# Attention with a relative bias, then a two-layer network: a change to the planner that writes out the order of the work

## The chip, the cores and the metric

The kernel runs on one core of a Trainium2 chip. The metric is device time in microseconds (us); lower is better. The engines are TensorE (PE in the profile, its weight loads PEld), VectorE (DVE), ScalarE (ACT), GpSimd (POOL) and SyncE (SP), which issues DMA transfers and computes nothing. Each has its own queue and works it off in order; semaphores tie them together.

## The reference, cut to what matters

```python
scores = scale * np.matmul(q, k.transpose(0, 1, 3, 2))     # q, k, v: 8 x 8 x 576 x 64
scores = scores + bias.transpose(2, 0, 1)[None, :, :, :]   # from a table of 32 buckets, by |i - j|
scores = scores - np.max(scores, axis=-1, keepdims=True)
attn = np.exp(scores)
attn = attn / (np.sum(attn, axis=-1, keepdims=True) + 1e-09)
out = np.matmul(attn, v)
x = np.ascontiguousarray(out.transpose(0, 2, 1, 3)).reshape(B * S, H * D)   # 4608 x 512
h = x @ w_in                                               # 512 x 2048
g = np.maximum(0.01 * h, h)
return (g @ w_out).astype(np.float32)                      # 2048 x 512
```

## The kernel before, in words

**Pairs.** Two heads of one batch are a pair; 8 batches make 32 pairs, numbered n = 0 to 31. For each pair, q and k (96 x 768 each, loaded by POOL's queue as bf16) must stand with the head's 64 numbers along the partitions, so they are turned. There are three ways. Pair 0 and pairs 5 to 7: `rows` (L362) copies the rows of both heads side by side into a tile `pr` (four buffers), six PE transposes for q and six for k turn it (`turn_by_pe`, L376), and `take_turned` (L393) copies the result from PSUM to `qt` and `kt`. Pairs 1 to 4: PE turns straight from the loaded rows (L381). From pair 8 on, `by_dma(n)` is true: `turn_by_dma` (L367) lets SP issue one DMA transpose from `pr` to `tu` for q and k together, and `take_turned` copies from `tu`, on DVE.

**Attention of a pair.** `score` (L418 to L426) makes six units of scores in PSUM, in two buffers `ps_s`; `expo` on ACT takes exp (L432, L434, L439); `band` on DVE multiplies the five blocks by the exp of the bias (L451); `av` (L471, L486, L489) multiplies by v with a column of ones; `norm` on DVE (L498, L499) divides into `opair`. The result is turned into `xT`, by PE (`x_pe`, L513, and a DVE copy `x_copy`, L517) for pairs 0 to 5 and two others, and by DMA (`x_dma`, L505, on SP) for the rest.

**The network.** Tokens go in nine blocks of 512. `ffn_in` (L529) makes 16 units of hidden values in PSUM tiles `pm`, ACT applies the leaky ReLU (L533), `ffn_out` (L557) multiplies by w_out, DVE copies (L562) and SP stores (L567). The PSUM pool M has three banks, and `pm`, one output of `av` (`ps_om`), and PE's transposes share it. The network's work is spread between the attention's, so that PE has something to do while ACT and DVE work on a pair.

**Who sets the order.** All engines run in an order written out when the program is built, by class `Plan`. Each piece of work is a task with an engine, a reckoned cost, a list of tasks that it comes after, a rank, and the PSUM slots that it takes and gives. `Plan.order` walks through a reckoned time: for each engine it finds the tasks that could start, takes the earliest (PE, before 34 us, may take a better rank that starts 0.3 us later), and notes start and end. A DMA transpose was reckoned to end 6 us after its issue (`tail=6.0`), whatever else the DMA rings carry; POOL's loads are reckoned to land one behind the other (`ring`). `Plan.run` then emits the tasks in that order, and, where PE is reckoned to be idle in the first 26 us, puts multiplications of a zero tile between (`spin`, L781), four of them ahead of all. The reckoned times go nowhere else: on the chip, only the order and the true data dependencies hold.

**Loads.** POOL issues the loads. Batches share two buffers, so the load of q and k of batch b comes after the rows of batch b - 2 were read, and in POOL's queue the order is: q and k of batch 2, v of batch 2, q and k of batch 3, v of batch 3, and so on; v of batch b comes after the last `av` of batch b - 2.

Of the kernel before, what the change touches and what calls it, by code (L numbers as in the profile page):

```python
# [36 lines left out]
class Plan:  # L37


    LAG, WARM, EARLY, PATIENCE = 0.25, 26.0, 34.0, 0.3  # L40

    def __init__(self, slots):
        self.tasks = []
# [3 lines left out]
    def add(self, engine, cost, after, go, rank, take=(), give=(), tail=0.0, at=None):  # L47
        t = {"engine": engine, "cost": cost, "after": list(after), "go": go, "rank": rank, "n": len(self.tasks),
             "take": list(take), "give": list(give), "tail": tail, "end": at, "start": at}
        if at is None:  # L50
            self.tasks.append(t)
        return t
# [8 lines left out]
    def order(self):  # L61

        free, done, waiting, ring = {}, [], {}, 0.0
        for t in self.tasks:
            waiting.setdefault(t["engine"], []).append(t)
        while any(waiting.values()):
            best = None
            for e, ts in waiting.items():
                now = free.get(e, 0.0)
                ready = []  # L70
                for t in ts:
                    if any(d["end"] is None for d in t["after"] + t["behind"]):
                        continue
                    r = now
                    for d in t["after"]:
                        r = max(r, d["end"] + (self.LAG if d["engine"] != e else 0.0))
                    for k in set(t["take"]):
                        s, m = sorted(self.slots[k]), t["take"].count(k)
                        r = max(r, s[m - 1]) if len(s) >= m else None
                        if r is None:  # L80
                            break
                    if r is None:
                        continue
                    ready.append((r, t["rank"], t["n"], t))
                if ready:
                    r = min(ready)[0]
                    slack = self.PATIENCE if e == "PE" and r < self.EARLY else 0.0
                    pick = min((rank, n, s, t) for s, rank, n, t in ready if s <= r + slack) if slack else None
                    pick = (pick[2], pick[0], pick[1], pick[3]) if pick else min(ready)
                    if best is None or pick[:3] < best[:3]:  # L90
                        best = pick
            assert best is not None, [(e, len(w)) for e, w in waiting.items()]
            r, t = best[0], best[3]
            e = t["engine"]
            waiting[e].remove(t)
            t["start"], t["end"] = r, r + t["cost"] + t["tail"]
            if "moves" in t:
                t["end"] = ring = max(ring, r + t["cost"] + 2.0) + t["moves"]
            t["idle"] = r - free.get(e, 0.0)
            free[e] = r + t["cost"]  # L100
            for k in t["take"]:
                self.slots[k].remove(min(self.slots[k]))
            for k in t["give"]:
                self.slots[k].append(t["end"] + self.LAG)
            done.append(t)
        return done

    def run(self, fill):

        for t in self.order():  # L110
            if t["engine"] == "PE" and 3.6 < t["start"] < self.WARM:
                k = int((t["idle"] - 0.3) / (0.45 if t["start"] < 8.0 else 0.25))
                if k > 0:
                    fill(k)
            t["go"]()
# [3 lines left out]
def kernel(  # L119
# [18 lines left out]
    n_pairs = H // 2  # L138
# [117 lines left out]
    spare = extra[:, 0 : ATW + SL], extra[:, ATW + SL : ATW + SL + S + SL]  # L256
# [86 lines left out]
    qts, kts, opairs, prs, turned, scores, outs = {}, {}, {}, {}, {}, {}, {}  # L343

    def by_dma(n):
        return n >= 2 * n_pairs

    def rows_by_pool(n):
        return False
# [4 lines left out]
    def rows(n, j):  # L354

        b, p = items[n]
        if j == 0:
            prs[n] = pr_pool.tile([RQ, 2, NC, 2 * D], BF16, name="pr")
        src = raw[:, j, :, :].rearrange("r e (c d) -> r e c d", d=D) if n == 0 else \
            (qn, kn)[j][b % NBUF][0:RQ, 2 * p : 2 * p + 2, :, :]  # L360
        copy = nc.scalar.copy if n + j == j == 1 else (nc.gpsimd if rows_by_pool(n) else nc.vector).tensor_copy
        copy(out=prs[n][:, j, :, :].rearrange("r c (e d) -> r c e d", e=2),  # L362
                        in_=src.rearrange("r e c d -> r c e d"))

    def turn_by_dma(n):
        t = turned[n] = tu_pool.tile([P, 2 * NC, RQ], BF16, name="tu")
        nc.sync.dma_start_transpose(out=t, in_=prs.pop(n).rearrange("r j c d -> r (j c d)"))  # L367
# [142 lines left out]
    def x_pe(n):  # L510
        ps = outs[n, "x"] = ps_m_pool.tile([P, 8 * P], BF16, name="ps_tx", tag="m")
        for ic in range(NJ + 1):
            nc.tensor.transpose(ps[:, ic * P : (ic + 1) * P], in_=opairs[n][:, ic, :], identity=ident)  # L513

    def x_copy(n):
        b, p = items[n]
        nc.vector.tensor_copy(out=xT[p][:, b * S : (b + 1) * S], in_=outs.pop((n, "x"))[:, 0:S])  # L517
# [52 lines left out]
    add = plan.add  # L570
    L = {}
    rowt, cut, sct, ext, avt, nrt, nmt, xt, vt = {}, {}, {}, {}, {}, {}, {}, {}, {}
# [52 lines left out]
    def plan_rows(n):  # L625
        b, p = items[n]
        rank = 10 * n
        feed = rank - (25 if n < n_pairs else 0)
        ld = None if n == 0 else (L["qk", 0, p - 1] if b == 0 else L["qk", b, p // 2])
        old = [t for t in rowt.get(n - 4, [])[2:]] + (nrt[n_pairs - 1] if n == n_pairs + 1 else [])  # L630
        on, cost = ("POOL", 0.9) if rows_by_pool(n) else ("DVE", 0.35)
        if n == 0:
            r0 = add("DVE", 0.6, [L["raw", 0]], lambda: rows(0, 0), feed)
            r1 = add("ACT", 0.75, [L["raw", 1]], lambda: rows(0, 1), feed)
        elif by_heads(n):
            r0 = r1 = ld
        else:
            r0 = add(on, cost, [ld] + old, lambda: rows(n, 0), feed)
            r1 = add(on, cost, [ld, r0], lambda: rows(n, 1), feed)
        wait = [("in", 0, 1)] if n == n_pairs + 1 else (sct[n - 2][-1:] if n > n_pairs + 1 else [])  # L640
        if by_dma(n):
            d = add("SP", 0.1, [r0, r1] + cut.get(n - 4, [])[:2], lambda: turn_by_dma(n), rank, tail=6.0)
            rowt[n] = [r0, r1, d]
            src, give = [d, d], []
        else:
            g = [add("PE", 0.4 if by_heads(n) else 0.28, [(r0, r1)[j]] + sct.get(n - NQT, []) + wait, lambda j=j: turn_by_pe(n, j), feed, take=["M"])
                 for j in range(2)]
            rowt[n] = g if by_heads(n) else [r0, r1] + g
            src, give = g, ["M"]
        behind = ext[n - 1] if n == n_pairs else []  # L650
        on_act = n < n_pairs - 1 or n_pairs <= n < 2 * n_pairs
        cq = add("ACT" if on_act else "DVE", 0.6 if on_act else 0.75, [src[0]] + behind + sct.get(n - NQT, []),
                 lambda c=nc.scalar.copy if on_act else nc.vector.tensor_copy: take_turned(n, 0, c), feed, give=give)
        on_act = n == n_pairs
        ck = add("ACT" if on_act else "DVE", 0.6 if on_act else 0.75, [src[1]] + behind + sct.get(n - NQT, []),
                 lambda: take_turned(n, 1, nc.scalar.copy if n == n_pairs else nc.vector.tensor_copy), feed, give=give)
        on, cost = ("POOL", 0.5) if 0 < n < n_pairs else ("DVE", 0.2)
        ak = add(on, cost, [ck], lambda: apart(n, kts[n]), feed + 1 if n != 1 else -7)
        aq = add(on, cost, [cq], lambda: apart(n, qts[n]), feed + 1 if n != 1 else -7)
        cut[n] = [cq, ck, aq, ak]  # L660
# [6 lines left out]
    def plan_pair(n):  # L667
        b, p = items[n]
        rank = 10 * n
# [41 lines left out]
        if x_by_dma(n):  # L711
            xt[n] = [add("SP", 0.1, nms, lambda: x_dma(n), soon + 4, tail=6.0)]
            nmt[n] = xt[n]
        else:
            xt[n] = [add("PE", 0.3, nms, lambda: x_pe(n), soon + 4, take=["M"])]
            nmt[n] = [add("DVE", 0.45, xt[n], lambda: x_copy(n), soon + 3, give=["M"])]

    def plan_loads(b):
# [59 lines left out]
    def spin(k):  # L778
        pw = ps_w_pool[0]
        for _ in range(k):  # L780
            nc.tensor.matmul(pw, lhsT=junk[:, 0:P], rhs=junk, start=True, stop=True)  # L781

    ps_w_pool = [ps_m_pool.tile([P, 512], FP32, name="ps_w", tag="m")]
    spin(4)
    plan.run(spin)


# [28 lines left out]
```

## Time and profile before

| What | Value |
|---|---|
| median of three runs | 382.77 us (382.54, 382.77, 387.25) |
| the profiled execution | 388.05 us |
| its span, first to last instruction | 386.1 us |
| PE busy | 370.4 us, 96% |
| ACT busy | 244.7 us, 63% |
| DVE busy | 205.6 us, 53% |
| mean granted TensorE clock | 0.991 |

The profiled execution is longer than its span by 1.95 us, and longer than the median by 5.28 us. In the views below, "timeline" rows give start and duration in us, engine, line, operation, output<-inputs, shapes, count, and in brackets the engine's idle time before and what ended it. A q behind an engine's name marks its queue's issue of a DMA.

### The profile page before, as it was taken

The page shows a single profiled execution, that of the slowest core. Times are in us where ns is not written, and L with a number is a line of the kernel's source. Part 1 is how long each engine was busy: PE and PEld are TensorE (multiplying, and loading weights), DVE is VectorE, ACT ScalarE, POOL GpSimd, SP SyncE. Part 2 cuts the span into 40 slices and gives each one's busy share as a digit, 9 for nine tenths or more (in the row PEclk, how much of TensorE's full clock was granted, in tenths as well). Part 3 has the DMA queues.
Part 4 walks back from the last instruction along what each step waited for, and adds up shares of the span by engine and source line. Part 5 has one row for each costly group of instructions (what it writes and reads, how often), then busy time and mean ns, then how long its engine had stood idle before and what let it go on. Part 6 is the DMA issues. An engine that isn't in the chain of part 4 may idle for free.

```text
span 386.1 us, 8513 instructions
## 1 busy us (share of the span) xinstructions
PE 370.4 (96%) x3469; PEld 191.2 (50%) x3509; DVE 205.6 (53%) x538; ACT 244.7 (63%) x352; POOL 80.2 (21%) x125
## 2 busy tenths in 40 slices
PE   8979999799799999999999999999999999999996
PEld 4547455454344455555555454555454644444444
DVE  7788566685666765757565656555534411001011
ACT  5877996459565798579758775877687533333300
POOL 8994732061003400510060004000000000000000
PEclk9989999999999999999999999999999999999999
DMA  8699999999936993997499839411111100101112
GB/s 153 134 201 220 206 195 143 184 117 159 167 64 114 151 176 58 106 200 122 55 117 152 140 80 107 76 46 44 47 46 44 47 29 27 56 27 42 41 54 82
DMA packets 95046, 40.82 MB, mean 106 GB/s; under 512 B 74304, under 2 KB 88928, under 8 KB 95008
## 3 DMA queue, kind: packets, MB, share of 16 engines
q0 software_dynamic: 44672, 19.24, 43.6%
q1 hardware_dynamic: 50128, 20.75, 27.4%
q8 instruction: 27, 0.44, 0.5%
q10 hardware_dynamic: 208, 0.29, 0.3%
q14 instruction: 11, 0.09, 0.1%
HBM read 36.70 MB, written 9.44 MB: 120 GB/s over the span
## 4 chain that ended last, share of the span: by engine, by line
PE 89%; DVE 6%; DMA 3%; issue 1%; ACT 0%; POOL 0%; POOLq 0%
PE pm L529 33%; PE pm L557 29%; PE ps_s L418 9%; PE ps_om L486 5%; PE ps_o L486 5%; DMA tu<-pr 3%; PE ps_s L422 2%; PE ps_s L425 2%; DVE at L451 1%; PE pm L541 1%; DVE kt L393 1%; PE ps_o L471 1%; PE ps_t L381 1%; PE ps_tx L513 1%; DVE opair L499 1%
## 5 line engine op out<-in xcount | busy, mean ns | idle before, releaser
L432 ACT ACTIVATE at<-ps_s 128x1024 bf16<-128x1024 f32 x124 | 121.0, 1033 | 36.8 <-PE ps_s L418 35.9
L529 PE MATMUL pm<-xT,w_in_sb 128*128 128x512 bf16 x550 | 140.2, 382 | 4.2 <-DVE opair L499 2.8
L557 PE MATMUL pm<-w_out_sb,gt 128*128 128x512 bf16 x549 | 133.6, 379 | 0.6
L533 ACT ACTIVATE gt<-pm 128x512 bf16<-128x512 f32 x144 | 84.3, 610 | 64.9 <-PE pm L529 62.0
L451 DVE TENSOR_TENSOR at<-at,hk 128x768 bf16<-128x768 bf16 (+3 forms) x155 | 70.0, 465 | 33.8 <-ACT at L432 27.0
L529 PEld LDWEIGHTS <-w_in_sb 128*128 128x128 bf16 x576 | 52.7, 98 | 68.3 <-issue 9.1
L557 PEld LDWEIGHTS <-gt 128*128 128x128 bf16 x560 | 52.4, 98 | 64.4 <-issue 4.7
L562 DVE COPY y<-pm 128x512 f32<-128x512 f32 x35 | 24.1, 689 | 70.0 <-PE pm L557 70.0
L199 POOL DMA_DIRECT2D vn<-in_v_dram x24 | 21.9, 940 | 145.5 <-PE ps_o L486 140.4
L418 PE MATMUL ps_s<-qt,kt 64*128 64x512 bf16 x256 | 42.1, 397 | 3.3 <-DVE kt L393 2.6
L486 PEld LDWEIGHTS <-at 128*128 128x128 bf16 x1240 | 41.6, 98 | 3.4 <-issue 1.5
L434 ACT ACTIVATE at<-ps_s 128x512 bf16<-128x512 f32 x31 | 18.6, 599 | 16.4 <-PE ps_s L422 11.5
L393 DVE COPY qt<-tu 128x576 bf16<-128x576 bf16 x24 | 16.9, 704 | 20.4 <-PE ps_s L426 11.0
L486 PE MATMUL ps_o<-vn,at 128*128 128x65 bf16 x640 | 25.8, 195 | 0.0
L486 PE MATMUL ps_om<-vn,at 128*128 128x65 bf16 x600 | 24.4, 195 | 0.3 <-issue 0.3
L498 DVE RECIPROCAL rcp<-ps_om 128x5 f32<-128x5 f32 x31 | 6.0, 195 | 33.0 <-PE ps_om L486 31.8
L418 PEld LDWEIGHTS <-kt 64*128 64x128 bf16 x256 | 8.3, 94 | 29.0 <-issue 24.9
L439 ACT ACTIVATE at<-ps_s 128x576 bf16<-128x576 f32 x31 | 20.3, 656 | 1.2 <-PE ps_s L426 1.0
L393 DVE COPY kt<-tu 128x576 bf16<-128x576 bf16 x24 | 17.0, 707 | 0.0
L499 DVE TENSOR_TENSOR opair<-ps_o,rcp 128x320 bf16<-128x320 f32 x33 | 16.2, 492 | 1.1
L499 DVE TENSOR_TENSOR opair<-ps_om,rcp 128x320 bf16<-128x320 f32 x31 | 15.2, 491 | 1.1
L191 POOL DMA_DIRECT2D kn<-in_k_dram x17 | 12.7, 747 | 5.3 <-DMA w_in_sb<-in_moe_w_in_dram 3.0
(98 smaller groups left out, 254.4 us busy)
## 6 DMA issues: line engine op xcount, KB each, us to landing
out_dram<-y SPq DMA_DIRECT2D x35, 256.0 KB, 2.0
qn<-in_q_dram POOLq DMA_DIRECT2D x14, 288.0 KB, 9.8
kn<-in_k_dram POOLq DMA_DIRECT2D x14, 288.0 KB, 11.5
vn<-in_v_dram POOLq DMA_DIRECT2D x24, 128.0 KB, 5.2
w_in_sb<-in_moe_w_in_dram POOLq DMA_DIRECT2D x2, 1024.0 KB, 11.9
w_out_sb<-in_moe_w_out_dram POOLq DMA_DIRECT2D x2, 1024.0 KB, 14.2
staged<-in_v_dram POOLq DMA_DIRECT2D x4, 256.0 KB, 12.1
first<-in_v_dram POOLq DMA_DIRECT2D x4, 192.0 KB, 4.6
```

The source lines that it names most:

```text
L199: nc.gpsimd.dma_start(out=vn[i][:, c, :, 0:D], in_=v[b, :, c * P : (c + 1) * P, :].rearrange("h s d -> s h d"),)
L393: copy(out=t[:, 0:S].rearrange("p (r c) -> p r c", c=NC), in_=src)
L418: nc.tensor.matmul(ps[:, e, :], lhsT=kt[r, u * P : (u + 1) * P], rhs=qt[r, 0:512], start=True, stop=True)
L432: nc.scalar.activation(at[:, :, u, 0:512], ps, AF.Exp, scale=scale)
L439: nc.scalar.activation(at4[:, 0:S], ps.rearrange("p e i -> p (e i)")[:, 0:S], AF.Exp, scale=scale)
L451: nc.vector.tensor_tensor(out=o, in0=o, in1=m, op=ALU.mult)
L486: nc.tensor.matmul(ps[:, ic, :], lhsT=at[:, o : o + P], rhs=vn[i][:, c, 2 * p + e, :], start=whole and c == 0, stop=not whole and ic == NJ ...
L499: nc.vector.tensor_tensor(out=opairs[n][:, :, e * D : (e + 1) * D], in0=ps[:, :, 0:D], in1=rcp.to_broadcast([P, NJ + 1, D]), op=ALU.mult)
L529: nc.tensor.matmul(pms[T, f], lhsT=w_in_sb[:, c, f * P : (f + 1) * P], rhs=xT[c][:, t0 : t0 + w], start=(c == 0), stop=(c == n_cc - 1))
L533: nc.scalar.activation(gts[T][:, f, :], pms.pop((T, f)), AF.Prelu, bias=0.0, scale=1.0, alpha=0.01)
L557: nc.tensor.matmul(ys[T, ts], lhsT=gts[T][:, f, ts * P : (ts + 1) * P], rhs=w_out_sb[:, f, :], start=(f == 0), stop=(f == n_fc - 1))
L562: nc.vector.tensor_copy(out=y, in_=ys[T, ts])
```

## The change

Six edits, all in the planner and in the tasks given to it. No arithmetic is changed.

1. Pair 8 is no longer turned by DMA: `by_dma` starts at pair 9, so pair 8 takes twelve PE transposes and two copies from PSUM.
2. A DMA transpose is marked `turns`. Its reckoned end is no longer issue + 6.1 us but the loads' reckoned last landing + 2 us, held between 4.5 and 11 us after the issue. The copies of a turned pair also come after a unit of the scores two pairs earlier (`behind`).
3. For pairs turned by DMA, the `rows` copies get a rank 40 lower (`early`), so they are put further ahead.
4. PE's transposes of the outputs of pairs 0 to 2 (`x_pe`) are reckoned ready 1.2 us later (`spare`).
5. PE's tasks that start before 7 us are reckoned at 1.8 times their cost (`COLD`).
6. The filling: five multiplications of the zero tile ahead of all instead of four, and another formula for their number before 8.5 us.

```diff
-    LAG, WARM, EARLY, PATIENCE = 0.25, 26.0, 34.0, 0.3
+    LAG, COLD, WARM, EARLY, PATIENCE = 0.25, 7.0, 26.0, 34.0, 0.3
...
-                        r = max(r, d["end"] + (self.LAG if d["engine"] != e else 0.0))
+                        r = max(r, d["end"] + (self.LAG + t.get("spare", 0.0) if d["engine"] != e else 0.0))
...
-            t["start"], t["end"] = r, r + t["cost"] + t["tail"]
+            cost = t["cost"] * (1.8 if e == "PE" and r < self.COLD else 1.0)
+            t["start"], t["end"] = r, r + cost + t["tail"]
+            if "turns" in t:
+                t["end"] = max(r + 4.5, min(ring + 2.0, r + 11.0))
...
-            if t["engine"] == "PE" and 3.6 < t["start"] < self.WARM:
-                k = int((t["idle"] - 0.3) / (0.45 if t["start"] < 8.0 else 0.25))
+            if t["engine"] == "PE" and 3.9 < t["start"] < self.WARM:
+                k = round(t["idle"] / 0.45) if t["start"] < 8.5 else int((t["idle"] - 0.3) / 0.25)
...
     def by_dma(n):
-        return n >= 2 * n_pairs
+        return n >= 2 * n_pairs + 1
...
+        early = rank - 40 if by_dma(n) else feed
...
-            r0 = add(on, cost, [ld] + old, lambda: rows(n, 0), feed)
-            r1 = add(on, cost, [ld, r0], lambda: rows(n, 1), feed)
+            r0 = add(on, cost, [ld] + old, lambda: rows(n, 0), early)
+            r1 = add(on, cost, [ld, r0], lambda: rows(n, 1), early)
...
             d = add("SP", 0.1, [r0, r1] + cut.get(n - 4, [])[:2], lambda: turn_by_dma(n), rank, tail=6.0)
+            d["turns"] = True
...
-        behind = ext[n - 1] if n == n_pairs else []
+        behind = ext[n - 1] if n == n_pairs else (sct[n - 1][:1] if n == 2 * n_pairs + 1 else sct[n - 2][1:2] if by_dma(n) else [])
...
             xt[n] = [add("PE", 0.3, nms, lambda: x_pe(n), soon + 4, take=["M"])]
+            if n < n_pairs - 1:
+                xt[n][0]["spare"] = 1.2
...
-    spin(4)
+    spin(5)
```

What this makes of the queues, in the program as built:

- **PE, start.** Five zero multiplications instead of four ahead of the bias table's first matmul (L295), three instead of two behind it; then 16 matmuls of the bias table (L311), pair 0's twelve transposes, and 32 more matmuls of the table, where 32 stood ahead of the transposes and 16 behind. Pair 2's k is turned ahead of the fourth score unit of pair 0, not behind its fifth.
- **PE, outputs of pairs 0 to 2.** `x_pe` of pair 0 stood ahead of score units 3 and 4 of pair 2, and now stands behind them; those of pairs 1 and 2 also come later.
- **PE, pair 8.** Its transposes stand behind the first two score units of pair 7.
- **DVE.** The rows of pair 9 stand ahead of those of pair 8. `take_turned` of pair 8 moves ahead of `band` 0 of pair 7. `take_turned` of pair 9 stands behind the last `band` of pair 7. The rows of pairs 12 to 15 move from the time of `band` 0 to 4 of pair 9 to that of pair 8 and the beginning of pair 9. `take_turned` of pair 12 stands behind `band` 1 of pair 10, where it stood ahead of `band` 0 of pair 10; for the later pairs q's copy stands ahead of, and k's behind, `norm` and `band` 2 of a pair.
- **SP.** One DMA transpose fewer; those of pairs 12 to 15 stand earlier among the stores.
- **POOL.** The memsets for batch 1's v stand ahead of its load instead of behind.

More of the change, by code (lines that the diff above doesn't have):

```diff
@@ L99, in order @@
             t["idle"] = r - free.get(e, 0.0)
-            free[e] = r + t["cost"]
+            free[e] = r + cost
             for k in t["take"]:
```

## The prediction

> **What bounds the kernel now.** I read the page's busy times and its chain that ended last, then PE's waits, then the timeline around each long wait, then windows around the dips of the clock.
>
> ```profile
> PE 370.4 (96%) x3469; PEld 191.2 (50%) x3509; DVE 205.6 (53%) x538; ACT 244.7 (63%) x352; POOL 80.2 (21%) x125
> PE 89%; DVE 6%; DMA 3%; issue 1%; ACT 0%; POOL 0%; POOLq 0%
> ```
>
> PE is busy 96% of the span and makes 89% of the chain: a microsecond counts only if PE loses it. What PE waits for is in its waits (total, times, longest):
>
> ```profile
> PE pm L529 <- DVE opair L499: 2.8, 1, 2.8
> PE ps_s L418 <- DVE kt L393: 2.6, 2, 2.1
> PE ps_tx L513 <- DVE opair L499: 2.1, 1, 2.1
> ```
>
> Three waits of over 2 us, each happening once. The clock adds to two of them (stretch, length, then PE, PEld, DVE, ACT, POOL busy, PEclk, DMA share and rate):
>
> ```profile
> 22.69:26.10 3.41, 1.58 (x13) 0.91 (x15) 3.38 (x11) 2.04 (x3) 3.33 (x6) 1.00 1.12 206
> 26.10:29.51 3.41, 3.39 (x42) 2.26 (x41) 2.14 (x7) 2.34 (x4) 3.31 (x7) 0.50 1.12 211
> 70.47:73.88 3.41, 2.24 (x15) 0.91 (x12) 0.87 (x2) 1.14 (x2) 0.00 (x0) 1.00 1.31 167
> 101.20:104.61 3.41, 0.84 (x4) 0.41 (x5) 3.34 (x13) 0.99 (x2) 0.00 (x0) 1.00 1.12 148
> 104.61:108.02 3.41, 3.41 (x11) 0.85 (x10) 3.31 (x11) 1.99 (x3) 0.00 (x0) 0.50 0.70 131
> ```
>
> A stretch with PE busy 1.58 or 0.84 of 3.41 us is followed by 3.41 us at half clock; one with 2.24 is not. From 104.61 on PE is full, so it loses half, 1.70 us.
>
> **Edit 4, `x_pe` later.**
>
> ```profile
> 19.81 2.41 DVE L451 TENSOR_TENSOR at<-at,hk 128x512 bf16<-128x512 bf16 x1
> 20.45 1.48 POOL L231 CAST vn<-first 128x1536 bf16<-128x1536 f32 x1
> 23.45 0.49 DVE L499 TENSOR_TENSOR opair<-ps_om,rcp 128x320 bf16<-128x320 f32 x1
> 24.00 0.45 PE L513 MATMUL ps_tx<-ident,opair 128*128 128x128 bf16 x5 [2.08 <-DVE opair L499]
> 24.82 1.02 ACT L432 ACTIVATE extra<-ps_s 128x1024 bf16<-128x1024 f32 x1 [1.37 <-PE ps_s L418]
> 29.06 1.02 ACT L432 ACTIVATE at<-ps_s 128x1024 bf16<-128x1024 f32 x1 [1.01 <-PE ps_s L418]
> ```
>
> One band takes 2.41 us beside POOL's cast, so pair 0's output is ready only at 23.94, with PE's next scores stuck behind its transposes and ACT idle 1.37 us for want of them. With the scores ahead, ACT goes on, and PE still ends this wait at 23.94 but with two score units done. The half clock at 26.10 costs ACT another 1.01 us. Until about 36 us this stage is carried by ACT and DVE in turn, so PE's 2.08 us are not won in full. ACT's idle time bounds the gain at 1.37 + 1.01 = 2.4; nothing is the other bound, since DVE is 3.38 of 3.41 us busy there; a loss is excluded, since nothing is added. I take 1.8 where the clock dips, three quarters, because both idle times end in front of the exps that the next pairs wait for; without the dip 1.0 (three quarters of 1.37).
>
> **Edits 1 and 2 at pair 8.**
>
> ```profile
> 62.40 6.96 SPq L367 DMA_TRANSPOSE tu<-pr  x2
> 62.64 0.67 POOL L191 DMA_DIRECT2D kn<-in_k_dram  x1 [1.19 <-DVE pr L362]
> 63.48 0.60 PE L418 MATMUL ps_s<-qt,kt 64*128 64x512 bf16 x4
> 73.01 0.64 DVE L393 COPY qt<-tu 128x576 bf16<-128x576 bf16 x1 [2.97 <-DMA tu<-pr]
> 74.86 0.61 PE L418 MATMUL ps_s<-qt,kt 64*128 64x512 bf16 x4 [2.15 <-DVE kt L393]
> DMA to landing us min/median/max: 10.4/10.4/10.4
> DMA to landing us min/median/max: 10.6/10.6/10.6
> DMA to landing us min/median/max: 3.3/3.9/10.5
> ```
>
> The three rows on landing are for batch 3's last load (issued at 62.64), for pair 8's transpose (62.40), and for the transposes after 110 us (minimum, median, maximum). Pair 8's took 10.6 us beside that load's 10.4; the later median is 3.9. PE wanted pair 8 at 74.86 - 2.15 = 72.71, when DVE did not have it yet. On PE this goes: -2.15. Pair 9's transpose is then the first of the burst and lands near 73.0; its copies stand in DVE's queue behind the last `band` of pair 7, and all of pair 8's scores stand ahead of pair 9's on PE: that covers the landing. If the cover were gone, the old 2.15 is the price again. What PE pays for pair 8:
>
> ```profile
> 50.19 0.67 PE L376 MATMUL ps_t<-ident,pr 96*128 96x96 bf16 x12
> 50.70 1.03 PE L529 MATMUL pm<-xT,w_in_sb 128*128 128x512 bf16 x3
> ```
>
> Twelve transposes hold PE 50.70 - 50.19 = 0.51 us when work follows, 0.67 at most: +0.6, on the path, because PE is full there. Their two PSUM banks are free while `ffn_out` works in the third. They start when pair 7's first scores end (63.48 + 0.60 = 64.1), and DVE copies them ahead of `band` 0 of pair 7, while `ffn_out` still has two parts to do in its own bank: no wait for a bank.
>
> **Edits 2 and 3 at pair 12: rows ahead, copies behind.**
>
> ```profile
> 80.39 3.83 POOL L199 DMA_DIRECT2D vn<-in_v_dram  x4 [17.08 <-PE ps_o L486]
> 87.73 0.70 POOL L191 DMA_DIRECT2D kn<-in_k_dram  x1
> 87.96 8.26 SPq L367 DMA_TRANSPOSE tu<-pr  x2
> 99.74 0.65 DVE L393 COPY qt<-tu 128x576 bf16<-128x576 bf16 x1 [6.42 <-PE pm L529]
> 103.22 0.49 DVE L499 TENSOR_TENSOR opair<-ps_om,rcp 128x320 bf16<-128x320 f32 x1
> 103.77 2.82 PE L529 MATMUL pm<-xT,w_in_sb 128*128 128x512 bf16 x8 [2.78 <-DVE opair L499]
> DMA to landing us min/median/max: 11.7/11.7/11.7
> ```
>
> Issued at 87.96, 0.23 us after the last of batch 4's loads, pair 12's transpose landed after 11.7 us, at 99.65. DVE stood 6.42 us before its copy (99.74), with pair 10's bands and pair 9's `norm` queued behind; PE ran out of PSUM banks until `norm` ended at 103.71. The name <-PE in the bracket is not the cause; the landing is. In the changed queues pair 12's rows stand right behind pair 9's copies, with batch 3's k landed at 62.64 + 10.4 = 73.0, so the transpose goes out near 77 (estimate: two copies of 0.65, two of rows, and SP's queue), ahead of the loads from 80.39 on. That is 11 us earlier. Its copies stand behind `band` 1 of pair 10, so it is also wanted later, by the two exps that these bands wait for (1.02 each). The earlier landing alone covers the 6.42. -2.78 for the wait and -1.70 for the half clock behind it.
>
> **What could be late next.** Copies of q now stand ahead of `norm` in each pair from 12 on, 0.65 us each:
>
> ```profile
> DVE rcp L498 <- PE ps_om L486: 28.0, 19, 2.7
> DVE pr L362 <- DMA kn<-in_k_dram: 3.4, 4, 1.2
> ```
>
> These are DVE's waits from 110 to 310 us. Before `norm` it idles 28.0 / 19 = 1.47 us, so 0.65 fits: 0. Rows wait for k's landing four times, at most 1.2 us, and PE never waited for that: 0. On SP, the transposes of pairs 12 to 15 now stand ahead of some stores and of an `x_dma`, which go out later, by up to half of 6.96 us for each: 0, as no wait of PE's names a store or `xT`. On POOL, memsets stand ahead of batch 1's v, which pair 4 is the first to use: 0.
>
> **Edits 5 and 6, the start.**
>
> ```profile
> 3.57 1.03 PE L781 MATMUL ps_w<-junk 128*128 128x512 bf16 x2
> 4.61 1.03 PE L311 MATMUL ps_us<-diag,hots 128*128 128x32 bf16 x32
> 5.74 1.14 PE L376 MATMUL ps_t<-ident,pr 96*128 96x96 bf16 x12
> 6.68 0.63 PE L311 MATMUL ps_u<-diag,hots 128*128 128x32 bf16 x16
> 7.73 0.61 PE L418 MATMUL ps_s<-qt,kt 64*128 64x512 bf16 x2 [0.43 <-DVE kt L393]
> ```
>
> A zero multiplication takes at most (4.61 - 3.57) / 2 = 0.52 us. Two more move the table's first matmuls from 4.61 to 5.65 at most; half of those, 0.52, no longer stand ahead of the transposes, but 1.03 of table work instead of 0.63 stands between them and the first score. That score comes at most 1.04 - 0.52 + 0.40 = 0.9 later, and about 0.3 if the 0.43 and 0.2 us that PE waited in these rows are filled. The table's last part, behind one more group of transposes, comes about 0.6 later. POOL's cast at 20.45 to 21.93 holds DVE until 22.14 either way and hides that: 0. Without the cover it is +0.6; a clock that is granted earlier could gain as much.
>
> **The sum.** Against the profiled execution: 388.05 - 1.8 - 2.15 - 2.78 - 1.70 + 0.6 = 380.2. That execution lies 5.28 above the median, 382.77. The half clock's stretches (1.70, and 0.8 through edit 4) are the only losses I can name that would differ from run to run; they explain half. So for the median I leave them out: 382.77 - 1.0 - 2.15 - 2.78 + 0.6 = 377.4.
>
> **Rivals.**
> A. The median's runs hold both half-clock stretches, and their 5.28 us lie elsewhere: 382.77 - 7.83 = 374.9, with 7.83 the sum's total. For: a wait of 2.08 us already brought the dip. Against: then nothing in the views explains the 5.28.
>
> The Trainium skill, "TensorE: Matmul & The Clock Gate", section "Why this matters for your kernels", advises to leave no gap of over about 3 us between bursts of matmuls, since one idle window brings the half clock back. By that rule waits of 2.08 and 2.78 us would bring nothing, the dips would have another cause and stay, and A would give the forecast's 377.4 (the profiled execution 382.7 instead of 380.2). The windows above disagree: with PE busy for 1.58 and 0.84 of 3.41 us, 0.50 followed.
>
> B. A wait returns: pair 12's stays because PE's banks, not the landing, hold it, or DVE's longer queue gives one like it: 377.4 + 2.78 = 380.2. For: DVE is busy 3.34 of 3.41 us from 101.20 on. Against: that is the backlog of its 6.42 us.
>
> C. Slower: rows copied ahead wait in DVE's queue for the loads of batches 4 to 7 and hold `norm` up, as at 99.74, at 2.78 + 1.70 = 4.48 each. One gives 381.9, two 386.4, slower than before from the second; by over 2% from the third, 390.8. Against: the four waits of rows for k were 1.2 us at most, and none reached PE.
>
> D. The change does not do what it says: the transposes still land behind loads and are wanted as early, so that half of the two waits stays: 382.77 - 1.0 - 2.47 + 0.6 = 379.9. For: the reckoned end is held to 11 us, and 11.7 was measured. Against: the queues as built put ten and more microseconds between.
>
> **How the numbers follow.** Forecast 0.50, A 0.20, B 0.13, C 0.06, D 0.11. The time is the forecast's, 377.4. The range goes from 374.4 (A, 374.9, with 0.5 for the start) to 380.8 (B, 380.2, with the start's 0.6); C and the odd ends stay out. Two per cent, about what a measurement of this kernel can tell from no change, is 375.1 and 390.4. Faster by more: most of A and a little of the forecast's lower end, 0.20. Slower by more: C with three stops, 0.03. Within: 0.77.
>
> **What would show it.** Right: no wait of `ps_s` for kt near 72, none of `pm` for opair near 100, no window at 0.50 after 16 us, PE busy up by about 0.6. Edit 4: ACT's idle time at 24.8 gone. Wrong: DVE waiting for `tu` or for kn with PE waiting right after; a first score after 8.6; a PE wait before L557 for the PSUM banks of pair 8.

## The result, and the profile after

| | before | after |
|---|---|---|
| median (lowest to highest), 20 runs each | 385.20 (382.54 to 388.66) | 380.54 (379.10 to 384.54) |
| ratio, 95% interval | | 0.990 [0.987, 0.993] |
| profiled execution; its span | 388.05; 386.1 | 380.86; 378.9 |

The change made the kernel 1.0% faster by the ratio, which leaves out runs more than 1.5% above a kernel's fastest. The forecast was 377.4, its range 374.4 to 380.8: the median lies in it, near its upper end. The three runs of before that it started from were a low draw (382.77; over 20 runs 385.20), which makes 2.4 of the 3.1 us that it missed by; that its working failed as well comes out below. Between the two profiled executions it foresaw 7.8 us and 7.2 came; this agreement is partly luck.

The page of after, busy times and chain; then PE's waits (total, times, longest):

```profile
PE 369.3 (97%) x3524; PEld 190.0 (50%) x3524; DVE 207.9 (55%) x538; ACT 243.8 (64%) x352; POOL 83.3 (22%) x125
PE 84%; DVE 8%; DMA 4%; ACT 3%; issue 1%; ACTq 0%
```

```profile
PE ps_tx L516 <- DVE opair L502: 1.0, 2, 0.8
PE ps_o L489 <- DVE opair L502: 1.0, 1, 1.0
PE ps_s L428 <- ACT at L435: 0.4, 1, 0.4
```

The waits of `pm` for opair near 100 us and of `ps_s` for kt near 72 are gone, and no window after 6.1 us shows half clock until the last matmuls. What is new stands in the timelines of DVE and PE:

```profile
73.26 0.65 DVE L396 COPY qt<-tu 128x576 bf16<-128x576 bf16 x1 [2.93 <-DMA tu<-pr]
76.94 0.49 DVE L502 TENSOR_TENSOR opair<-ps_om,rcp 128x320 bf16<-128x320 f32 x1
78.12 0.45 PE L516 MATMUL ps_tx<-ident,opair 128*128 128x128 bf16 x5 [0.84 <-DVE opair L502]
```

DVE stands 2.93 us for pair 9's DMA transpose. Pair 7's `norm` is queued behind its copies, and PE waits 0.84 us for that `norm`. This is the sign that the prediction named as wrong: DVE waiting for `tu`, PE waiting right after.

### The profile page after: what moved, and what is told of

Its sections match the earlier page's. It is cut to its first block, busy times and chain, and to the rows that moved or that the text cites. A ratio compares the mean times of both kernels' runs of the same rounds, so it can differ in the third digit from the quotient of the medians.

```text
span 378.9 us, 8582 instructions
## 1 busy us (share of the span) xinstructions
PE 369.3 (97%) x3524; PEld 190.0 (50%) x3524; DVE 207.9 (55%) x538; ACT 243.8 (64%) x352; POOL 83.3 (22%) x125
## 4 chain that ended last, share of the span: by engine, by line
PE 84%; DVE 8%; DMA 4%; ACT 3%; issue 1%; ACTq 0%
PE pm L532 31%; PE pm L560 29%; PE ps_s L421 7%; PE ps_om L489 5%; PE ps_o L489 4%; DMA tu<-pr 4%; DVE at L454 3%; PE ps_s L425 2%; PE ps_s L428 1%; DVE opair L502 1%; PE ps_w L788 1%; ACT at L435 1%; PE pm L544 1%; DVE pr L365 1%; PE ps_o L474 1%
## 5 line engine op out<-in xcount | busy, mean ns | idle before, releaser
L560 PE MATMUL pm<-w_out_sb,gt 128*128 128x512 bf16 x560 | 135.3, 379 | 0.0
L454 DVE TENSOR_TENSOR at<-at,hk 128x768 bf16<-128x768 bf16 (+3 forms) x155 | 73.1, 479 | 56.4 <-ACT at L435 41.2
L421 PE MATMUL ps_s<-qt,kt 64*128 64x512 bf16 x256 | 40.0, 381 | 0.9 <-ACT extra L435 0.3
L396 DVE COPY qt<-tu 128x576 bf16<-128x576 bf16 x23 | 14.9, 648 | 2.9 <-DMA tu<-pr 2.9
L396 DVE COPY kt<-tu 128x576 bf16<-128x576 bf16 x23 | 14.8, 644 | 0.0
L425 PEld LDWEIGHTS <-kt 128*128 128x128 bf16 x128 | 9.5, 98 | 7.2 <-ACT at L435 0.5
```

The source lines that it names most:

```text
L396: copy(out=t[:, 0:S].rearrange("p (r c) -> p r c", c=NC), in_=src)
L421: nc.tensor.matmul(ps[:, e, :], lhsT=kt[r, u * P : (u + 1) * P], rhs=qt[r, 0:512], start=True, stop=True)
L454: nc.vector.tensor_tensor(out=o, in0=o, in1=m, op=ALU.mult)
L560: nc.tensor.matmul(ys[T, ts], lhsT=gts[T][:, f, ts * P : (ts + 1) * P], rhs=w_out_sb[:, f, :], start=(f == 0), stop=(f == n_fc - 1))
```

## The experiments

The kernels ran in five groups (e1 to e4; e5, e7 to e9; e10 to e13; e14 to e16; e17 to e19), each on one chip with runs of before beside it. A run's mean granted clock tells whether it held a stretch of 3.41 us at half clock: 0.998 and more is none. In 135 runs of before this sorts the times:

| mean clock of the run | runs of before | mean time |
|---|---|---|
| 0.998 to 1.000 | 46 | 381.61 |
| 0.994 to 0.997 | 39 | 383.86 |
| 0.989 to 0.993 | 40 | 386.69 |
| below | 10 | 389.10 |

A stretch goes with about 2.5 us more. The half clock itself can take half of 3.41, 1.70 us, so the rest lies in the waits that come with it. Below, "clean" means runs without one, and "to before" is the mean of the clean runs less that of before's clean runs on the same chip (381.42, 381.72, 382.08, 381.31 and 381.43 in the five groups).

| kernel | median (range) | runs | clean: number, mean | to before | ratio [95%] |
|---|---|---|---|---|---|
| e1, edit 1 alone | 384.6 (381.6 to 388.5) | 12 | 2, 383.05 | +1.6 | 1.006 [1.002, 1.009] |
| e2, edits 2 and 3 | 382.15 (380.9 to 383.3) | 12 | 3, 381.18 | -0.2 | 0.997 [0.994, 1.000] |
| e3, edits 5 and 6 | 386.3 (382.0 to 390.0) | 12 | 1, 382.98 | +1.6 | 1.004 [0.999, 1.009] |
| e4, edit 4 | 384.3 (381.5 to 387.0) | 12 | 5, 382.35 | +0.9 | 1.002 [0.997, 1.006] |
| e5, all but edit 1 | 380.89 (379.8 to 384.0) | 12 | 11, 380.75 | -1.0 | 0.996 [0.993, 0.999] |
| e7, before, filled | 383.3 (381.9 to 390.7) | 12 | 9, 383.20 | +1.5 | 1.003 [0.999, 1.006] |
| e9, after, pair 9's copies later | 379.62 (378.8 to 381.4) | 12 | 12, 379.62 | -2.1 | 0.992 [0.990, 0.994] |
| e10, all but edit 4 | 380.56 (379.2 to 384.1) | 12 | 5, 379.91 | -2.2 | 0.993 [0.988, 0.997] |
| e11, all but edit 3 | 379.82 (379.0 to 380.4) | 8 | 8, 379.72 | -2.4 | 0.992 [0.990, 0.995] |
| e12, all but edit 2 | 383.59 (379.8 to 385.1) | 12 | 6, 381.20 | -0.9 | 0.999 [0.994, 1.004] |
| e13, after again | 381.93 (379.3 to 384.4) | 12 | 9, 380.89 | -1.2 | 0.996 [0.992, 1.001] |
| e14, edit 2 alone | 382.15 (379.9 to 385.1) | 12 | 4, 380.99 | -0.3 | 0.997 [0.993, 1.002] |
| e15, edits 1 and 2 | 379.47 (378.1 to 383.8) | 6 | 3, 378.40 | -2.9 | 0.990 [0.983, 0.997] |
| e16, e11 and e9's edit | 379.39 (378.9 to 379.8) | 6 | 6, 379.34 | -2.0 | 0.990 [0.984, 0.996] |
| e17, e18 and filling | 379.75 (377.8 to 381.8) | 12 | 9, 379.17 | -2.3 | 0.990 [0.986, 0.994] |
| e18, e15 and e9's edit | 380.13 (377.8 to 383.7) | 12 | 5, 378.32 | -3.1 | 0.991 [0.987, 0.995] |
| e19, e18 and edit 4 | 379.23 (378.3 to 380.2) | 6 | 6, 379.18 | -2.2 | 0.990 [0.984, 0.995] |

**One edit at a time: e1 to e4.** Each is before with the hunks of the diff that its edits name, for e1:

```diff
-        return n >= 2 * n_pairs
+        return n >= 2 * n_pairs + 1
```

For e2, e3 and e4 one line of each stands for the hunks of its edits:

```diff
+                t["end"] = max(r + 4.5, min(ring + 2.0, r + 11.0))
...
+            cost = t["cost"] * (1.8 if e == "PE" and r < self.COLD else 1.0)
...
+                xt[n][0]["spare"] = 1.2
```

> Before, with edit 1 alone (pair 8 turned by PE). My sum: PE's wait of 2.15 us for pair 8's kt goes and twelve transposes cost 0.5, so -1.6 us against before; the wait of 2.78 us for opair near 100 us and the half clock behind it stay. Rival: pair 9's transpose, now first behind batch 3's loads, holds DVE's queue in the same place (its copies stand ahead of the last bands of pair 7), and PE waits for that instead: 0 or worse.

> Before, with edits 2 and 3 alone (transposes reckoned behind loads, rows ahead), pair 8 still turned by DMA. My sum: the wait of 2.78 near 100 us and the 1.7 of half clock go, and PE's queue has more of the network's work ahead of pair 8's scores, so most of the 2.15 goes too: -4.5 to -6.6 us. Rival: pair 8 cannot be had before its landing, other work runs out, and the 2.15 moves: -4.5 at most; or the wait near 100 us belongs to PSUM banks and stays: 0 to -2.

> Before, with edits 5 and 6 alone (start: three more zero multiplications by count, another order of the table and the first transposes). My prediction: 0, at most +0.6. Rival, from the trace of the changed kernel, where half clock ends at 6.09 us and not at 15.86: the start's clock is granted earlier and pair 1's scores begin 1.5 us earlier: -1.5 us, up to -2.6 by pair 4.

> Before, with edit 4 alone (x_pe of pairs 0 to 2 reckoned 1.2 us later). My sum: -1.0 without a dip of the clock, -1.8 with it, PE's wait of 2.08 near 22 us gone. Rival: this stage is held by DVE behind POOL's cast, and the order of PE's work there is worth nothing: 0, and the gain at pair 4 in the changed kernel comes from the start's clock alone.

No edit alone brings the gain of all. Edit 1 alone only hands the wait on. In its timeline DVE (the first row is pair 9's copy, the next two are pair 10's) and in PE's waits:

```profile
71.80 0.66 DVE L393 COPY qt<-tu 128x576 bf16<-128x576 bf16 x1 [3.42 <-DMA tu<-pr]
74.93 0.65 DVE L393 COPY qt<-tu 128x576 bf16<-128x576 bf16 x1 [0.95 <-DMA tu<-pr]
76.90 0.64 DVE L393 COPY kt<-tu 128x576 bf16<-128x576 bf16 x1
77.68 0.49 DVE L499 TENSOR_TENSOR opair<-ps_om,rcp 128x320 bf16<-128x320 f32 x1
```

```profile
PE ps_tx L513 <- DVE opair L499: 2.9, 2, 2.0
```

Now the copies of pairs 9 and 10 stand in DVE's queue ahead of pair 7's `norm`, and PE waits 2.0 us for that instead. Edits 2 and 3 put pair 8's scores later in PE's queue, so its landing no longer matters; the runs draw together (382.15), yet 9 of 12 hold a stretch (in the profiled one near 23 us).

**Before once more: e8.** No edit.

> The kernel before, unchanged, looked at once more. Theory P: the three waits (near 22, 72 and 100 us, 2.1 to 2.8 us each) stand in every run, and only the half-clock stretches of 3.41 us behind them come and go; so whatever the time, three waits of about 2 us or more stand in the trace, 7.0 us together, and the time is 381.3 without a stretch, about 384 with one, 386.5 with two. Rival Q: the waits themselves come and go; a run near 381 then shows waits of less than 1 us at two of the three places, and a run of 386 all three.

It took 382.23 us without a stretch. PE's waits:

```profile
PE ps_s L418 <- DVE kt L393: 3.3, 2, 2.8
PE ps_tx L513 <- DVE opair L499: 1.3, 2, 0.9
PE pm L529 <- DVE opair L499: 0.6, 1, 0.6
```

In this run rival Q is right: two of the three waits are below 1 us. Of theory P, only the wait for pair 8's kt stands (2.8); the other two, 2.1 and 2.8 in the execution that I predicted from, are 0.9 and 0.6 here. Why the one near 22 us changes shows in the timelines of DVE and POOL, e8 first, then e18, which has the same order of work there:

```profile
19.67 0.70 DVE L451 TENSOR_TENSOR at<-at,hk 128x768 bf16<-128x768 bf16 x1
20.51 0.49 DVE L499 TENSOR_TENSOR opair<-ps_om,rcp 128x320 bf16<-128x320 f32 x1
20.91 2.93 DVE L451 TENSOR_TENSOR at<-at,hk 128x768 bf16<-128x768 bf16 x2
21.40 1.48 POOL L231 CAST vn<-first 128x1536 bf16<-128x1536 f32 x1
```

```profile
19.35 2.40 DVE L453 TENSOR_TENSOR at<-at,hk 128x512 bf16<-128x512 bf16 x1
19.98 1.48 POOL L233 CAST vn<-first 128x1536 bf16<-128x1536 f32 x1
22.99 0.49 DVE L501 TENSOR_TENSOR opair<-ps_om,rcp 128x320 bf16<-128x320 f32 x1
23.54 0.72 PE L515 MATMUL ps_tx<-ident,opair 128*128 128x128 bf16 x5 [2.71 <-DVE opair L501]
```

A band that meets POOL's cast takes over 2 us. In e8 pair 0's `norm` is done before the cast begins, in e18 a band ahead of that `norm` is caught. Which of the two happens goes with the moment at which the trace first shows the full clock granted. In the ten traces with the old place of pair 0's `x_pe` (e7 aside, whose filling covers the wait) it was 5.4 to 7.0 us in four (before again, e1, e3, e10: waits 0.79 to 0.89) and 9.1 to 15.9 in six (before, e2, e14, e15, e18, and e17 with its filling counted: waits 1.83 to 2.72). The queues ahead of it were the same in before and e8, where that moment was 15.86 and 5.45: it changes from run to run by itself. Not every longer wait brings a stretch: e14's, 1.83, brought none.

**Filled waits: e7.** Before, with multiplications of the zero tile in the two waits:

```diff
+        if n == 2 * n_pairs and u == 0:           # in score()
+            for _ in range(8):
+                nc.tensor.matmul(ps[:, 0, :], lhsT=junk[:, 0:P], rhs=junk, start=True, stop=True)
+        if n == 0:                                # in x_pe()
+            spin(8)
```

> The kernel before with eight multiplications of the zero tile added ahead of pair 0's x_pe and eight ahead of pair 8's first scores, 8 x 0.22 = 1.8 us each, so that TensorE is busy in the waits near 22 and 72 us and loses nothing as long as these waits last that long. Theory P (a stretch at half clock follows a window of 3.41 us in which TensorE was mostly idle): the stretches near 26 and 74 us go, that behind the wait near 100 us stays possible; the median falls from 384.4 to 382 to 383, and over half of the runs show a clock of 0.999 or more (before 13 of 35). Rival: the stretches have another cause than TensorE's idle time; then 384.4 as before, ratio 1.000, and a clock of 0.996 or less in two thirds of the runs. Rival Q (waits shorter than 1.8 us in many runs): up to 3 us slower in those runs, lowest time over 382.

The share of clean runs rose from 13 of 29 to 9 of 12, as theory P says, but the clean runs became 1.5 us longer. In its trace `opair` is ready at 20.93 and the filling ends only at 21.92, so the first wait is shorter than its filling; and at 80.91 PE waits 1.92 us for `opair`, where e8 has 0.41. How the 1.5 us divide between the two is not shown. The same number of microseconds without work does not always bring a stretch. Windows on the trace's grid of 3.41 us, first e8, then e3 (columns as in the prediction):

```profile
66.89:70.31 3.42, 2.46 (x16) 1.03 (x13) 0.00 (x0) 1.14 (x2) 0.00 (x0) 1.00 1.43 140
70.31:73.72 3.41, 1.56 (x9) 0.62 (x10) 2.63 (x7) 1.13 (x2) 0.00 (x0) 1.00 1.28 170
73.72:77.14 3.42, 3.42 (x58) 2.04 (x56) 2.69 (x7) 2.12 (x3) 0.00 (x0) 1.00 1.16 187
```

```profile
70.25:73.66 3.41, 0.91 (x6) 0.33 (x7) 2.63 (x7) 0.48 (x1) 0.00 (x0) 1.00 1.24 184
73.66:77.07 3.41, 3.41 (x10) 1.21 (x8) 2.01 (x4) 1.46 (x2) 0.00 (x0) 0.50 1.18 197
```

The same wait, 2.82 and 2.92 us, lies across two windows in e8 and nothing follows; in e3 most of it lies in one, and half clock follows. In all traces a window at full clock with PE busy up to 1.31 us was followed by half clock, one of 1.91 and more never; between, two were (1.58 in before, 1.77 in e10) and two were not (1.56 in e8, 1.59 in e1). Within a stretch the same work keeps PE busy longer: windows at half clock with 2.33 (e18), 2.46 (e4) and 2.83 us (e15) were followed by a second one, those with 2.91 (e2) and more by full clock.

**One edit left out: e5, e10, e11, e12, with e13 as their base** (e5 ran in another group). Each is after with that edit's hunks undone.

> The changed kernel with pair 8 turned by DMA again (edit 1 undone, edits 2 to 6 kept). If edit 1 is worth its wait less its transposes in the presence of the rest (2.15 - 0.6), the median is 380.5 + 1.5 = 382.0, and a wait for kt of about 2 us stands near 70 us, with a half-clock stretch behind it in a part of the runs (spread up to 385). Rival: edits 2 and 3 do it all, because pair 8's copies or its scores come later in the queues; then the median is 380.5 or 0.6 less, 379.9, with all runs within 379 to 383, and the turns-only kernel's 382.15 lacks the other edits.

> The changed kernel without edit 4: x_pe of pairs 0 to 2 stands early in TensorE's queue again. If edit 4 is what keeps the first half-clock stretch away, a wait of 1 to 2.7 us ahead of pair 0's x_pe near 20 us is back, a stretch near 23 to 26 us follows it in more than half of the runs, and the median is 381.5 to 382.5, about 1.5 over the changed kernel's. Rival: the stretches went with the waits near 70 and 100 us alone, and edit 4 does nothing: the changed kernel's median within 0.4, with one run in five at a clock below 0.998.

> The changed kernel without edit 3: rows are copied as early as before, the transposes keep their new reckoned end and their copies the later place. If the rows ahead are what brings pair 12's transpose ahead of batch 4's loads, its transpose goes out near 85 us behind them again, lands after 95, and a wait of TensorE's for a PSUM bank near 97 to 100 us returns with 0.6 to 2.8 us: median 381.5 to 383. Rival: the later place of the copies alone covers the late landing; then no wait over 0.5 us near 98 and the changed kernel's median within 0.4.

> The changed kernel without edit 2: a DMA transpose is reckoned to end 6 us after its issue and its copies are not put behind scores, but rows are copied ahead and pair 8 is turned by TensorE. If the new reckoning is what counts, DVE stands for pair 9's landing and then for pair 12's, TensorE waits 1 us or more near 77 and near 98, and the median is 382 or more. Rival: rows ahead alone give the early landing, and the copies' place hardly matters: the changed kernel's median within 0.5.

> The changed kernel unchanged, as the base of the three kernels beside it: 380.5, with four runs in five at a clock of 0.998 or more and within 379 to 382.5; the few others above 383.

- e13, the base, has a ratio of 0.996 [0.992, 1.001]: on that chip the gain of the whole change can't be told from no gain.
- Without edit 1 (e5) the median is 380.89, 11 of 12 runs are clean, and no wait for kt stands near 70 us: the rival, not the expected 382.0.
- Without edit 2 (e12) the gain is gone: the median lies 1.7 us above e13's, and half of the runs hold a stretch. DVE, standing for pair 9's transpose, and PE, in the timeline and in the waits:

```profile
75.36 0.65 DVE L394 COPY qt<-tu 128x576 bf16<-128x576 bf16 x1 [7.28 <-DMA tu<-pr]
```

```profile
PE ps_o L472 <- DVE at L452: 3.4, 1, 3.4
```

- Without edit 3 (e11) it is better: 379.82 against 381.93 on the same chip, and all eight runs within 1.4 us. The rows ahead were not needed for pair 12: in e11 its transpose goes out at 85.27 and lands after 11.8 us, as late as in before, and PE has no wait there, as the rival said. And they bring pair 9's copies up to `band` 0 of pair 8. How long DVE stands there changes from run to run. After's profiled execution, then e13's: the DMA view of pair 9's transpose (issued at 59.49 and 59.56; last column us to landing), and DVE's copy in e13:

```profile
tu<-pr SPq DMA_TRANSPOSE x1, 13.8
```

```profile
tu<-pr SPq DMA_TRANSPOSE x1, 10.6
```

```profile
70.22 0.64 DVE L396 COPY qt<-tu 128x576 bf16<-128x576 bf16 x1
```

With 10.6 us there is no wait at all in e13, and its span is 1.0 us shorter (377.8 against 378.9). That can be part of the 4.0 us between after's clean runs (379.10 to 383.06): e9, e11, e16 and e19, where DVE stands there for 0.5 us at most, keep within 2.6, 1.4, 1.0 and 1.9 us.

- Without edit 4 (e10) the clean runs are 1.0 us shorter, and 7 of 12 hold a stretch (in the profiled one near 23 us). The median of all, 380.56, is 1.4 below e13's and that of after's 32 runs on two occasions, 380.60; the loss of about 1.5 that I expected did not come.

**Edit 2, alone and with edit 1: e14 and e15.**

> The kernel before with edit 2 alone: the DMA transposes' new reckoned end and their copies behind scores; pair 8 stays with DMA, rows stay where they were. If edit 2 is the whole change, the median is 380 to 381, no wait for kt stands near 70 us, none for a PSUM bank near 98, and over half of the runs show a clock of 0.998 or more. Rival: without rows ahead pair 12's transpose lands late and the bank wait of 0.6 to 2.8 us returns, or without edit 4 the wait near 20 us with its half-clock stretch stays: 382 to 383.

> The kernel before with edits 1 and 2. If pair 8 by TensorE costs its 0.6 and saves nothing beside edit 2, the median is 0.6 over that with edit 2 alone. Rival: it still saves a wait for pair 8's late landing, 0.5 to 1.5 us, and the median is that much below.

Edit 2 alone is not the whole change: 382.15, and 0.3 us in clean runs. With edit 1 beside it, on the same chip, clean runs go from 380.99 (four runs) to 378.40 (three), more than I expected. In e14's timelines of DVE and PE:

```profile
72.17 0.65 DVE L395 COPY qt<-tu 128x576 bf16<-128x576 bf16 x1 [1.83 <-DMA tu<-pr]
80.86 0.45 PE L515 MATMUL ps_tx<-ident,opair 128*128 128x128 bf16 x5 [1.07 <-DVE opair L501]
```

DVE stands for pair 8's transpose, and PE waits for pair 7's `norm`. Neither wait is in e15's trace; they explain 1.1 us of the 2.6, and the rest stays open. Alone edit 1 gave nothing (e1), and beside edits 2 to 6 hardly anything (to before, -1.2 with it in e13, -1.0 without it in e5). Each of the two takes a wait that stood in the other's way (e1 and e14 show which), and edit 3 gives part of it back.

**Further versions: e9, e16, and e17 to e19.** The edit of e9, and the filling of e17:

```diff
-        behind = ext[n - 1] if n == n_pairs else (sct[n - 1][:1] if n == 2 * n_pairs + 1 else ...
+        behind = ext[n - 1] if n == n_pairs else (nrt[n - 2][-1:] if n == 2 * n_pairs + 1 else ...
```

```diff
+        if n == 0:                                # in x_pe()
+            spin(4)
```

> The changed kernel with one edit: pair 9's copies out of the DMA transpose come after pair 7's norm instead of after pair 8's first score unit, so that DVE no longer stands 2.93 us for their landing ahead of bands 0 and 1 of pair 8 and of that norm. If this wait costs PE its 0.84 us ahead of pair 7's x_pe, the median is 380.5 - 0.8 = 379.7. Rival: the copies come too late for pair 9's first scores, and PE waits there instead: 380.5 to 381.5, with a wait of ps_s for kt near 80 us.

> The changed kernel without edit 3, and with pair 9's copies behind pair 7's norm. Where DVE no longer stands for a landing near 70 us, dip-free runs agree within 1 us: median 379.3 to 379.9, all runs below 381, as for the two kernels that made one of these edits each. Rival: the two do not add, because pair 9's copies come too late for its scores: 380.5, with a wait for kt near 79 us.

> The kernel before with edits 1 and 2, pair 9's copies behind pair 7's norm, and four zero multiplications, 4 x 0.22 = 0.9 us, ahead of pair 0's x_pe; the start and the x_pe tasks stay as before. If the half-clock stretch near 23 us follows a window of 3.41 us with TensorE busy for less than about 1.8, 0.9 us more of work in the wait of 0.9 to 2.7 us keeps it away at no cost: over 8 runs in 10 at a clock of 0.998 or more, and a median of 378.4 to 378.9. Rival: the stretch comes anyway, in about half of the runs as without the filling, and the median is 379.5 or more.

> The same without the filling, as its control: about half of the runs with a half-clock stretch near 23 us and 1.5 to 2.5 us longer for it, the others at 378.4; median 379 to 380.

> The control with edit 4: x_pe of pairs 0 to 2 later. If edit 4 trades the stretch near 23 us for a cost of its own of about 1 us (alone it made the runs without a stretch 0.9 longer; without it the changed kernel's were 1.0 shorter), nearly all runs are without a stretch and the median is 379.4. Rival: it costs nothing, and the rest of the start (edits 5 and 6) is what costs: median 378.4.

e9 and e16 came out as expected (379.62 and 379.39). e18, the control, is the fastest in clean runs (378.32), but 7 of 12 runs hold a stretch. Filling 0.9 us (e17) brings clean runs to 9 of 12, which so few runs can't set apart from 5 of 12, and edit 4 (e19) to 6 of 6; each costs clean runs 0.85 us: the filling is not free, as I had expected it to be. The window ahead, in e18 and in e17:

```profile
19.38:22.79 3.41, 1.31 (x24) 0.68 (x20) 3.38 (x6) 2.90 (x4) 3.27 (x5) 1.00 1.25 201
22.79:26.20 3.41, 2.33 (x13) 1.42 (x15) 3.36 (x10) 1.36 (x2) 3.41 (x6) 0.50 1.12 210
```

```profile
19.60:23.01 3.41, 1.91 (x20) 0.77 (x17) 3.34 (x6) 2.69 (x3) 3.27 (x5) 1.00 1.21 194
23.01:26.43 3.42, 2.45 (x23) 1.28 (x24) 3.42 (x9) 2.07 (x4) 3.42 (x6) 1.00 1.12 204
```

The wait itself is about as long (2.71, and 0.81 of filling with 1.74 behind it). PE's work in the window rises from 1.31 to 1.91, and the half clock stays away. e11 beats after on one chip. e16 and e19 have ratios of 0.990 and runs that stay together, but after's own ratio in the result is 0.990 too, and they did not run beside it: that they are faster than after is not shown.

## Why the prediction was wrong, point by point

**The step that failed** is the move from the profiled execution to the median: "So for the median I leave them out: 382.77 - 1.0 - 2.15 - 2.78 + 0.6 = 377.4." I took the stretches out of the base and kept waits in the sum, in full, that a run without stretches need not have: in e8, the one clean execution of before with a trace, they are 0.89, 2.82 and 0.63 us, not 2.08, 2.15 and 2.78. 382.77 is near a clean run (381.61 on average). Of the kernel before, 89 of 135 runs are not clean, and its median over all is 384.02. From a clean base the terms are:

| term | predicted | measured in clean runs | from |
|---|---|---|---|
| edit 4 | -1.0 | +0.9 | e4 +0.9; e13 less e10 +1.0; e19 less e18 +0.9 |
| pair 8, with its transposes | -1.55 | -2.36 | pair 7's to pair 8's first score 12.04 in e8, 9.68 in after |
| wait near 100 us | -2.78 | -0.63 | e8's wait |
| edit 3, pair 9's copies | 0 | +1.2 | e13 less e11 |
| sum on 381.61 | | 380.7 | after's 26 clean runs: 380.56 |

The rows of pair 8 and of the wait near 100 us rest on single executions, but a third kernel bears their sum out: e15, with edits 1 and 2 alone, is 2.9 us shorter in clean runs, and the two rows add up to 3.0. That the whole sum meets 380.56 so closely is partly luck, as the other two are differences of means that are about half a microsecond uncertain.

The rest of the gain is in the stretches: 89 of 135 runs held one before, 6 of 32 after. Means over all runs go from 384.32 to 381.14; 1.05 of these 3.18 us are between clean runs, and 2.1 are stretches that no longer come. (The forecast's gain was 5.4; between the medians of the result it is 4.7.) So rival A was right in saying that the median's runs hold stretches (at the median over all, 384.02, one by the table above, not both), and wrong in its time, since its waits were those of a run with stretches too.

**Edit 4.** "a loss is excluded, since nothing is added" was wrong: a moved instruction keeps waiting what stands behind it. My sign for it failed as well. ACT's idle time in after:

```profile
24.84 0.65 ACT L442 ACTIVATE extra<-ps_s 128x576 bf16<-128x576 f32 x1 [1.67 <-PE ps_s L429]
28.61 1.94 ACT L435 ACTIVATE at<-ps_s 128x1024 bf16<-128x1024 f32 x2 [1.22 <-PE ps_s L421]
```

It is 1.67 and 1.22, where it was 1.37 and 1.01. The price shows later, in the network's matmuls between the first scores of pairs 11 and 12, in after and in e10 (without edit 4; stretch, length, then PE, DVE and ACT busy on `pm`, PEclk, DMA share and rate):

```profile
99.04:109.07 10.03, 7.41 (x33) 0.69 (x1) 1.74 (x4) 1.00 0.52 101
```

```profile
98.27:107.44 9.17, 6.33 (x28) 0.69 (x1) 1.25 (x3) 1.00 0.43 87
```

The two differ by 0.86 us, one unit of four matmuls (the fifth is a record missing in e10). With `x_pe` early, PE has done that unit by then at no cost; that it does so in its idle time in the first 50 us is argued from the queues, not shown. What edit 4 buys is the stretch near 23 us, which I had counted only for the profiled execution.

**Pair 8, edits 1 and 2.** Mechanism right, and its size too small. The cover ("that covers the landing") held for pair 9's scores and failed for pair 7's `norm`, which stands behind the copies: 0.84 us in after.

**Pair 12.** Right in what happens. The transpose went out where the prediction put it, near 77, and landed 8.9 us later, in the SP timeline and DMA view of after:

```profile
77.11 2.78 SPq L370 DMA_TRANSPOSE tu<-pr  x1
```

```profile
tu<-pr SPq DMA_TRANSPOSE x1, 8.9
```

The size held for one execution alone: the wait was 2.78 in before, 1.88 in e3 and 0.63 in e8, where the transpose landed 6.2, 5.3 and 4.0 us after pair 10's first score; e7, with the order of before there, has none. And the landing is not what needed edit 3: e11 has no wait there either. Rival D does not hold.

**The start.** Right: the first score came at 7.55, not after 8.6. That pair 1 began 1.52 us earlier in after is not edits 5 and 6: it began 1.81 earlier in e8, the kernel before. So before's profiled execution was slow at the start by itself, by its late first full clock (15.86), and the wait of 2.08 and the stretch at 26 us came with it; without this luck 7.8 and 7.2 would not have met. What edits 5 and 6 cost or bring, e3 (one clean run, +1.6) cannot say; it stays open.

**Rivals B and C.** A wait did return, at B's place in the argument (DVE's queue), for a third of B's price. C's rows waited for their loads 1.2 us at most in after (at 94.44), as in before, and no wait of PE's follows; where PE did wait, it was behind copies.

**The clock page.** The Trainium skill, "TensorE: Matmul & The Clock Gate", section "What's actually happening", says that the activity window is 3413 ns long and free-running. The traces agree: the stretches last 3.41 or 6.83 us, they begin and end on one grid of 3.41 us in each trace, and the same wait of 2.8 to 2.9 us brings one or not by where it lies. The section "Why this matters for your kernels" of the same page of the Trainium skill warns of gaps over about 3 us. Here a stretch followed gaps of 2.08 us (before), 2.71 (e18) and 2.92 (e3), and once several small ones of at most 0.86 (e10).

## What to carry to other kernels

Before you add up a profiled execution's waits, find out whether they belong to the run that you forecast. A wait that one late engine meets by chance and the half clock behind it can come and go together, so don't take one out and leave the other in, and look at the spread of many runs first. A planner's edit that moves copies ahead should be followed to whatever stands behind them in that queue. And an edit can be worth a cost in quiet runs if it keeps a rare loss away: compare runs with and without that loss separately.

## What the runs showed of the hardware

- The moment of the first full clock differs from run to run of one program: 15.86 and 5.45 us in before, 6.09 and 13.76 in after. In before's profiled execution PE was busy 2.89, 3.42 and 3.06 us in the three windows of 3.41 us ahead of 15.86; two score matmuls took 0.61 us until then and 0.39 after.
- In the profiled executions of e18 and e17, 0.6 us more of work in one window (1.31 against 1.91) went with 6.83 us at half clock or none.
- A DMA transpose issued at the same point landed after 13.8 or 10.6 us. POOL's last load of k around it landed after 14.0 and 9.2 us; that these loads hold the transpose is argued, not shown.
- One of DVE's bands (128x512) took 0.41 us ahead of POOL's cast (e8) and 2.40 across it (e18).
